# Token scores set between the parts of the value projection, and a stop for filler work at a product's end, in a recurrent-memory transformer layer

## The chip, the cores and the metric

The kernel runs on one core of a Trainium2 chip. Its time is the device time of one execution in microseconds; less is better. The core has five engines that run side by side, each through its own list of instructions in order: TensorE (PE, with its weight loads PEld), VectorE (DVE), ScalarE (ACT), GpSimd (POOL) and SyncE (SP), which here starts DMAs.

## The reference

One layer of a transformer with a recurrent memory: 2048 tokens of 640 values, in 64 segments of 32 tokens. Before each segment stand 8 memory rows, and the memory of the next segment is what attention gives for these 8 rows. Behind it comes a dense part with a squared ReLU.

```python
mem = mem0
for s in range(n_seg):                       # 64 segments, in order
    xs = x[:, s * seg_len:(s + 1) * seg_len]  # of the normalised input
    h = concatenate([mem, xs], axis=1)        # 8 + 32 rows
    q, k, v = h @ Wq, h @ Wk, h @ Wv          # 32 heads of 128
    scores = q @ k.T * scale                  # causal mask, memory seen by all
    o = (softmax(scores) @ v) @ Wo
    mem = o[:, :M]                            # the next segment's memory
    outs.append(o[:, M:])
h = x + concatenate(outs)
out = h + (relu(layernorm(h) @ w1 + b1) ** 2) @ w2 + b2
```

Segment s + 1 needs the memory of segment s, so the 64 steps form one chain.

## The kernel before, in words

The program is unrolled, and the order of each engine's instructions is that in which the Python code writes them; semaphores are added where one engine needs another's result. One call of `step(b, sp)` handles one segment s = 4b + sp. The rows that depend on the memory and the first 24 tokens ("main" rows) are handled in the step; projections of each segment's last 8 tokens ("tail" rows), which no memory needs, are prepared in blocks and used as filler.

In a step PE works through these groups. A "projection" is 20 matmuls: five chunks of the contraction, four matmuls in each, which fill the four 32-row quarters of a PSUM bank.

- Projections (line 234): q of head half 0 (`ps<-wq,hT`), k half 0 (`pk`), q half 1 (`px<-wq`), k half 1 (`ps<-wk`).
- `scores(0)` (line 495): 16 small matmuls, the scores of the memory rows for half 0, into the tile `sm`. Line 501 (DVE), 504 (ACT) and `soft2`, `soft3` (lines 510 to 529 on DVE, ACT and POOL) make the softmax of it and lay it out as `pB`.
- The value projection of half 0 (`px<-wv`), which ACT copies out in line 595, then the first chunk of half 1 (`ps1`, shown as `ps<-wv`).
- `scores(1)`, the same for half 1. It needs the transposed k of half 1 (line 485 on DVE). Its softmax ends with line 521 on DVE.
- The other four chunks of `ps1`; ACT copies the result out in line 614.
- `token_scores(0)` and `token_scores(1)` (line 587): 16 matmuls each, the scores of the 24 + 8 token rows, into a tile `sk` of their own. They need qT and kT, of which POOL puts in the tail rows (line 389). Their softmax (lines 618, 647 to 664) is wanted only in the next step.
- `values(0)` and `values(1)` (lines 537 and 542): probabilities times values for the memory rows; line 244 and 246 copy the result to `oT`.
- `pw` (line 270): 64 matmuls, the output projection of the memory rows. From it ACT and DVE make the next memory and write it, transposed, to `hT` (line 380), for which the next step's first projection waits.
- Token values of the step before (lines 421 and 426).

Filler stands in between. `portion` hands each step about 8 units; a unit is one chunk (4 matmuls) of a tail projection (`hTt`), or a tenth of a tail output projection (`wo,oTt`), and a product has 5 or 10 units. A half of the step's units goes ahead of `values(1)`: about a quarter ahead of `values(0)`, a quarter between the two, and the rest behind `pw`. `run(q, n, held, stop)` takes n units; with `stop` it breaks off when a unit ends a product.

All projections that go through `mmtile()` share three PSUM buffers: k half 1, `ps1`, `sk`, and the filler's products. A product that starts in a step takes the buffer that was filled and emptied first, in many steps that of `ps1`, and then waits for ACT's copy in line 614. `sk` is given back by line 649 on DVE, which stands behind `values(1)`.

Of the kernel before, what the change touches and what calls it, by code (L numbers as in the profile page):

```python
# [16 lines left out]
def kernel(  # L17
# [206 lines left out]
    def proj(w, by, lhs, n, ps, c0, c1):  # L224

        if by == "columns":
            wr = w[:].rearrange("p (c g j n k e) -> p c n k g j e", c=DC, g=G, n=2, j=4, k=4)
        elif by == "half":
            wr = w[:].rearrange("p (c k j n e) -> p c n k j e", c=DC, k=G, n=2, j=4)
        else:  # L230
            wr = w[:].rearrange("p (c k n f) -> p c n k f", c=DC, k=G, n=2)
        for c in range(c0, c1):
            for k in range(4):
                nc.tensor.matmul(ps[32 * k:32 * k + 32, :], lhsT=lhs(c), rhs=wr[:, c, n, k], start=(c == 0), stop=(c == DC - 1))  # L234

    def mmtile():
        return mm.tile([128, 512], F32, tag="mm", name="ps")
# [54 lines left out]
    fill, late, mid, nook = [], [], [], []  # L292

    def run(q, n, held=None, stop=False):
        while n > 0 and q:
            out = q.pop(0)()
            if out and held is not None:
                held.append(out)
                if stop:
                    break  # L300
            elif out:
                out[1]()
            n -= 1
# [10 lines left out]
    def settle(held, tails):  # L314
        for out in [o for o in held if o[0] == tails]:
            held.remove(out)
            out[1]()
# [96 lines left out]
    def token_values(s, v, vt4, po):  # L414

        sp = s % 4
        pTk, pTx = back.pop()
        for i in range(HG):
            for g in range(G):
                r = slice(32 * g, 32 * g + 32)  # L420
                nc.tensor.matmul(po[0][g][:, i * 32:(i + 1) * 32], lhsT=v[r, i * E:(i + 1) * E], rhs=pTk[r, i, :],  # L421
                                 start=(i == 0), stop=False, skip_group_check=True)
        for u in range(2):
            for g in range(G):
                r = slice(32 * g, 32 * g + 32)
                nc.tensor.matmul(po[0][g][:, u * 128:(u + 1) * 128].rearrange("p (j q) -> p j q", q=32)[:, :, 0:TL],  # L426
                                 lhsT=vt4[r, sp, u, :], rhs=pTx[r, u], start=False, stop=True, skip_group_check=True)

    def token_out(s, po):
        for h in range(2):  # L430
            gs = slice(2 * h, 2 * h + 2)
            nc.scalar.copy(out=oTg[:, gs, :, :, 0:SEG],  # L432
                           in_=po[1][h][:, :, 0:256].rearrange("p g (n j q) -> p g n j q", n=2, q=32))
        nc.gpsimd.tensor_copy(out=oTts[s // 4 % 2][:, :, s % 4 * TL:(s % 4 + 1) * TL], in_=oT[:, :, 0:TL])
# [17 lines left out]
    def step(b, sp, v=None):  # L452
        s = b * 4 + sp
        last = s == NS - 1
# [77 lines left out]
        def values(n, pB, po):  # L532
            cols = po[:, 0, 0:128]
            for j in range(4):
                i = n * 4 + j
                for k in range(4):
                    nc.tensor.matmul(cols[32 * k:32 * k + 32].rearrange("p (g i m) -> p i g m", g=G, i=4)[:, j],  # L537
                                     lhsT=v[:, i * E + 32 * k:i * E + 32 * k + 32],
                                     rhs=pB[:, :, SEG + j * M:SEG + (j + 1) * M],
                                     start=(j == 0), stop=False, skip_group_check=True)  # L540
            for k in range(4):
                nc.tensor.matmul(cols[32 * k:32 * k + 32].rearrange("p (g a) -> p g a", g=G), lhsT=vt4[:, sp, n, 32 * k:32 * k + 32], rhs=pB[:, :, 0:SEG],  # L542
                                 start=False, stop=True, skip_group_check=True)

        def values_out(n, po):
            evac(n == 1, oT[:, n * 16:(n + 1) * 16, SEG:NK], po[:, 0, 0:128].rearrange("p (a m) -> p a m", m=M))
# [28 lines left out]
        if not ready:  # L575
            ps0 = potile(0)
            proj(wv, "half", lhs, 0, ps0, 0, 2)
        sk = mmtile() if last else None

        def view():  # L580
            return sk[:, 0:HG * NK].rearrange("p (i k) -> p i k", k=NK)

        def token_scores(n):
            skv = view()
            for j in range(4):
                for g in range(G):
                    nc.tensor.matmul(skv[32 * g:32 * g + 32, n * 4 + j, :], lhsT=qT[:, n * 16 + g * 4 + j, :],  # L587
                                     rhs=kT[:, n * 16 + g * 4 + j, :], start=True, stop=True,
                                     skip_group_check=True)

        if last:
            token_scores(0)
        if not ready:
            proj(wv, "half", lhs, 0, ps0, 2, DC)
            nc.scalar.copy(out=v[:, 0:512], in_=ps0[:])
# [6 lines left out]
            pT0 = soft3(pm0)  # L602
        if not ready:
            proj(wv, "half", lhs, 1, ps1, 1, 2)
        if last:
            token_scores(1)
        if not ready:
            proj(wv, "half", lhs, 1, ps1, 2, DC)
        if not last:
            sk = mmtile()  # L610
            token_scores(0)
            token_scores(1)
        if not ready:
            nc.scalar.copy(out=v[:, 512:1024], in_=ps1[:])
        if not last:
# [1 line left out]
        def causal(skv):  # L617
            nc.vector.tensor_tensor(out=skv[:, :, M:NK], in0=skv[:, :, M:NK],
                                    in1=mask[:].unsqueeze(1).to_broadcast([128, HG, SEG]), op=ALU.add)

        held = []
# [5 lines left out]
        if last:  # L627
            run(fill, max(1, (len(fill) - 3) // 2), held, True)
            token_values(s - 1, *prevs[-2], po)
            token_out(s - 1, po)  # L630
            settle(held, True)
            run(fill, 2, held)
            settle(held, True)
            causal(skv)
        else:
            ahead = 0 if ready else (len(fill) + 1) // 2
            run(fill, ahead // 2, held)
            values(0, pT0, po[1][0])
            values_out(0, po[1][0])
            run(fill, ahead - ahead // 2, held)  # L640
            values(1, pT1, po[1][1])
            causal(skv)
            values_out(1, po[1][1])
            settle(held, True)
# [21 lines left out]
        if not last:  # L666
# [10 lines left out]
            held = []  # L677
# [236 lines left out]
    for b in range(NB):  # L914
        for sp in range(4):
# [34 lines left out]
            if 2 <= e <= NK4 + 1:  # L950
                late.insert(0, (1.15, lambda e=e: prep_stats0(e - 2), b * 4 + sp))
                mid.append(lambda e=e: prep_norm0(e - 2))
            step(b, sp, v0 if b + sp == 0 else None)

    def end_tails():
# [122 lines left out]
```

## Time and profile before

| what | value |
|---|---|
| times of three runs | 964.37, 963.79, 960.19 us; median 963.79 us |
| the profiled execution's own time | 961.72 us |
| its span (first to last instruction) | 959.9 us |
| around the span | 1.8 us |
| mean granted TensorE clock | 0.998 |
| PE busy | 927.6 us, 97% of the span |
| DVE, ACT, POOL busy | 701.8, 555.2, 312.3 us |
| step of the recurrence, for example | 452.4 to 464.3 us of the span: 11.9 us |

The page gives busy times, the chain of waits that ended last, and the costliest groups by source line. The timeline lists instructions in order of time, merged when equal ones follow each other: start, duration, engine, line, operation, tiles and shapes, count, and in brackets the idle time before with what ended it. A matmul's end is modelled; a row of 16 matmuls lasts to the modelled end of the last, so the time that a group takes from PE is the distance from its start to the start of the next PE row. "Issue" as the end of an idle time means that no semaphore explains it.

### The profile page before, as it was taken

The page shows a single profiled execution, that of the slowest core. Times are in us where ns is not written, and L with a number is a line of the kernel's source. Part 1 is how long each engine was busy: PE and PEld are TensorE (multiplying, and loading weights), DVE is VectorE, ACT ScalarE, POOL GpSimd, SP SyncE. Part 2 cuts the span into 40 slices and gives each one's busy share as a digit, 9 for nine tenths or more (in the row PEclk, how much of TensorE's full clock was granted, in tenths as well). Part 3 has the DMA queues.
Part 4 walks back from the last instruction along what each step waited for, and adds up shares of the span by engine and source line. Part 5 has one row for each costly group of instructions (what it writes and reads, how often), then busy time and mean ns, then how long its engine had stood idle before and what let it go on. Part 6 is the DMA issues. An engine that isn't in the chain of part 4 may idle for free.

```text
span 959.9 us, 55964 instructions
## 1 busy us (share of the span) xinstructions
PE 927.6 (97%) x24749; PEld 554.5 (58%) x24760; DVE 701.8 (73%) x2131; ACT 555.2 (58%) x1460; POOL 312.3 (33%) x1002
## 2 busy tenths in 40 slices
PE   5979999999999999999999999999999999999998
PEld 2436565656565656655565556666656655555555
DVE  5177887778877887877878787878787788556632
ACT  2546666666666666665666666666665665523321
POOL 2123333333333333333333333333333333353300
PEclk9999999999999999999999999999999999999999
DMA  9983201010102000100101010201020221633320
GB/s 354 403 258 66 43 16 27 16 31 13 23 19 29 16 21 24 21 25 9 36 9 31 15 31 14 32 12 33 9 31 8 53 43 21 208 101 87 94 56 28
DMA packets 65875, 56.66 MB, mean 59 GB/s; under 512 B 37384, under 2 KB 61712, under 8 KB 63712
## 3 DMA queue, kind: packets, MB, share of 16 engines
q1 hardware_dynamic: 65392, 52.74, 19.7%
q8 instruction: 194, 3.18, 1.4%
q14 instruction: 49, 0.40, 0.1%
q0 software_dynamic: 224, 0.33, 0.1%
q10 hardware_dynamic: 16, 0.01, 0.0%
HBM read 38.37 MB, written 9.44 MB: 50 GB/s over the span
## 4 chain that ended last, share of the span: by engine, by line
PE 87%; DMA 5%; DVE 3%; ACT 2%; SPq 2%; issue 1%; POOL 0%; ACTq 0%; DVEq 0%
PE ps L234 28%; PE pw L270 15%; PE px L234 13%; PE pk L234 7%; PE y L1035 6%; PE ps L983 6%; PE ps L270 3%; DMA wq<-in_A_Wq_dram 2%; PE po L421 2%; SPq L151 2%; PE po L537 2%; PE sm L495 1%; PE ps L587 1%; DMA wo<-in_A_Wo_dram 1%; PE po L542 1%
## 5 line engine op out<-in xcount | busy, mean ns | idle before, releaser
L234 PEld LDWEIGHTS <-hT 128*32 128x32 bf16 x7680 | 187.3, 96 | 179.4 <-DVE hT L380 23.0
L270 PE MATMUL pw<-wo,oT 128*32 128x320 bf16 x4224 | 160.5, 299 | 5.7 <-issue 3.3
L270 PEld LDWEIGHTS <-oT 128*32 128x32 bf16 x4224 | 120.2, 96 | 27.7 <-issue 9.4
L258 DVE STREAM_TRANSPOSE qT<-row 128x512 bf16<-128x512 bf16 x128 | 89.5, 699 | 44.7 <-ACT row L253 44.6
L234 PE MATMUL ps<-wv,hT 128*32 128x512 bf16 x1260 | 89.4, 378 | 0.0
L660 POOL TENSOR_TENSOR pkt<-ek,rk 128x64 bf16<-128x64 bf16 x64 | 19.0, 296 | 212.6 <-ACT otmp L286 142.5
L234 PE MATMUL ps<-wq,hT 128*32 128x512 bf16 x1260 | 81.6, 383 | 3.3 <-DVE hT L380 2.8
L654 ACT ACTIVATE ek<-tk 128x320 bf16<-128x320 f32 x64 | 30.1, 471 | 89.7 <-DVE tk L649 89.7
L234 PE MATMUL ps<-wk,hT 128*32 128x512 bf16 x1280 | 80.3, 379 | 0.0
L234 PE MATMUL px<-wq,hT 128*32 128x512 bf16 x1260 | 79.2, 379 | 0.0
L234 PE MATMUL px<-wv,hT 128*32 128x512 bf16 x1260 | 79.0, 378 | 0.0
L234 PE MATMUL pk<-wk,hT 128*32 128x512 bf16 x1240 | 77.9, 379 | 0.0
L991 ACT ACTIVATE wv<-ps,b1f 128x512 bf16<-128x512 f32 (+1 forms) x56 | 37.6, 672 | 67.0 <-PE ps L983 66.5
L432 ACT CAST oT<-po 128x512 bf16<-128x512 f32 x128 | 68.7, 589 | 8.2 <-PE po L426 2.5
L234 PEld LDWEIGHTS <-hTt 128*32 128x32 bf16 x1920 | 53.3, 97 | 32.3 <-issue 8.7
L441 POOL COPY qz<-qT 128x96 bf16<-128x96 bf16 x126 | 33.7, 267 | 112.0 <-DVE qT L258 112.0
L285 ACT COPY otmp<-pw 64x96 f32<-64x96 f32 (+2 forms) x129 | 28.9, 224 | 59.6 <-PE pw L270 39.0
L1035 PE MATMUL y<-wq,wk 128*128 128x320 bf16 x416 | 58.9, 299 | 0.2 <-DVE wk L992 0.2
L482 ACT CAST row<-ps 128x256 bf16<-128x256 f32 x126 | 40.8, 375 | 29.9 <-PE ps L234 29.1
L253 ACT ACTIVATE row<-ps 128x512 bf16<-128x512 f32 x93 | 54.7, 611 | 5.5 <-PE ps L234 4.4
L253 ACT ACTIVATE row<-px 128x512 bf16<-128x512 f32 x63 | 37.6, 597 | 32.2 <-PE px L234 32.2
L287 DVE TENSOR_TENSOR o<-pw,otmp 128x96 bf16<-128x96 f32 (+2 forms) x129 | 31.4, 243 | 31.5 <-ACT otmp L286 25.9
(138 smaller groups left out, 1887.5 us busy)
## 6 DMA issues: line engine op xcount, KB each, us to landing
wv<-in_A_Wv_dram SPq DMA_DIRECT2D x5, 1024.0 KB
wq<-in_A_Wq_dram SPq DMA_DIRECT2D x5, 1024.0 KB
wk<-in_A_Wk_dram SPq DMA_DIRECT2D x5, 1024.0 KB
wo<-in_A_Wo_dram SPq DMA_DIRECT2D x8, 640.0 KB
o_all<-o SPq DMA_DIRECT2D x256, 7.5 KB
vt<-vt_d SPq DMA_DIRECT2D x60, 64.0 KB
xt<-in_A_x_dram SPq DMA_DIRECT2D x19, 160.0 KB
wq<-in_B_w_dram SPq DMA_DIRECT2D x1, 2080.0 KB
```

Source lines behind the costliest of these rows:

```text
L234: nc.tensor.matmul(ps[32 * k:32 * k + 32, :], lhsT=lhs(c), rhs=wr[:, c, n, k], start=(c == 0), stop=(c == DC - 1))
L253: nc.scalar.mul(out=row, in_=ps, mul=scale)
L258: nc.vector.transpose(out=dst[:, n * 16:(n + 1) * 16, 0:32], in_=row.rearrange("p (h e) -> p h e", e=32))
L270: nc.tensor.matmul(pw[32 * j:32 * j + 32, c0:c0 + DH], lhsT=lhs(p), rhs=wov2[:, head(p), ch], start=(h == 0), stop=(h == 15))
L287: nc.vector.tensor_tensor(out=five(o[:])[:, cs], in0=blocks(0, 128, 32)[:, cs], in1=five(tmp[:])[:, cs], op=ALU.add)
L432: nc.scalar.copy(out=oTg[:, gs, :, :, 0:SEG], in_=po[1][h][:, :, 0:256].rearrange("p g (n j q) -> p g n j q", n=2, q=32))
L441: nc.gpsimd.tensor_copy(out=d.rearrange("p a (j f) -> p a j f", j=3)[:, :, :, 0:M], in_=src[:, :, 0:3, :])
L482: nc.scalar.copy(out=row[:, u * 256:(u + 1) * 256], in_=ps[:, u * 256:(u + 1) * 256])
L654: nc.scalar.activation(out=ek[:], in_=tk[:], func=ACT.Exp, scale=1.0)
L983: nc.tensor.matmul(ps[:], lhsT=w1[:, c, fc * 128:(fc + 1) * 128], rhs=hnT[:, c, :], start=(c == 0), stop=(c == DC - 1))
L991: nc.scalar.activation(out=r[:, 0:w], in_=ps[:, 0:w], func=ACT.Relu, bias=b1f[:, fc:fc + 1], scale=1.0)
L1035: nc.tensor.matmul(y[hh][:, 0:DH], lhsT=f1T[:, fc, k * 128:(k + 1) * 128], rhs=w2[:, fc, cs], start=(fc == 0 and not hf), stop=(fc == FFUL ...
```

## The change

Four edits, all in `step`:

- `sk` is taken from the three buffers ahead of `ps1`, in every step.
- `token_scores(0)` moves from behind `ps1` to between chunk 2 and chunk 3 of the value projection of half 0, ahead of `scores(1)`; `token_scores(1)` moves to between chunk 2 and chunk 3 of half 1. The last step had this order already.
- The filler ahead of `values(0)` stops when a product ends; what it left is made up between `values(0)` and `values(1)`, so that as many units as before stand ahead of `values(1)`.

```diff
-        sk = mmtile() if last else None
+        sk = mmtile()
...
-        if last:
-            token_scores(0)
+        token_scores(0)
         if not ready:
             proj(wv, "half", lhs, 0, ps0, 2, DC)
...
         if not ready:
             proj(wv, "half", lhs, 1, ps1, 1, 2)
-        if last:
-            token_scores(1)
+        token_scores(1)
         if not ready:
             proj(wv, "half", lhs, 1, ps1, 2, DC)
-        if not last:
-            sk = mmtile()
-            token_scores(0)
-            token_scores(1)
...
             ahead = 0 if ready else (len(fill) + 1) // 2
-            run(fill, ahead // 2, held)
+            left = len(fill) - ahead
+            run(fill, ahead // 2, held, True)
             values(0, pT0, po[1][0])
             values_out(0, po[1][0])
-            run(fill, ahead - ahead // 2, held)
+            run(fill, len(fill) - left, held)
             values(1, pT1, po[1][1])
```

The order of the instructions on DVE, ACT, POOL and SP is the same in both programs; PE's alone differs, with the same matmuls and weight loads.

## The prediction

> **What bounds the kernel now.** I read the page's busy times and its chain first, then the timeline of one usual step, then PE's waits over the 62 usual steps (62 to 818 us of the span).
>
> ```profile
> span 959.9 us, 55964 instructions
> PE 927.6 (97%) x24749; PEld 554.5 (58%) x24760; DVE 701.8 (73%) x2131; ACT 555.2 (58%) x1460; POOL 312.3 (33%) x1002
> PEclk9999999999999999999999999999999999999999
> PE 87%; DMA 5%; DVE 3%; ACT 2%; SPq 2%; issue 1%; POOL 0%; ACTq 0%; DVEq 0%
> ```
>
> PE is busy for 97% of the span at an undisturbed clock and carries 87% of the chain. The change keeps every matmul, so it can only gain what PE waits for, or what a packet of small matmuls costs more in one place than in another. Those few per cent lie in the middle of a step. The timeline's columns are start and duration in us, then the instruction, its count, and the idle time before:
>
> ```profile
> 456.81 0.27 PE L495 MATMUL sm<-kT,qz 128*32 128x40 bf16 x16
> 456.91 1.25 PE L234 MATMUL px<-wv,hT 128*32 128x512 bf16 x20
> 457.44 0.77 DVE L485 STREAM_TRANSPOSE kT<-row 128x256 bf16<-128x256 bf16 x2
> 457.89 0.31 POOL L389 COPY qT<-qTt 128x128 bf16<-128x128 bf16 x1
> 457.99 0.39 PE L234 MATMUL ps<-wv,hT 128*32 128x512 bf16 x4
> 458.20 0.33 PE L495 MATMUL sm<-kT,qz 128*32 128x40 bf16 x16
> 458.36 1.04 PE L234 MATMUL ps<-wv,hT 128*32 128x512 bf16 x16
> 458.59 0.20 DVE L501 TENSOR_REDUCE mx<-sm 128x1 f32<-128x40 f32 x1
> 459.08 0.56 POOL L529 COPY pB<-pT 32x64 bf16<-32x64 bf16 x2 [0.89 <-DVE pT L526]
> 459.21 0.42 PE L587 MATMUL ps<-kT,qT 128*32 128x40 bf16 x32
> 459.46 0.63 PE L234 MATMUL ps<-wk,hTt 128*32 128x512 bf16 x8
> 459.56 0.59 ACT L614 CAST v<-ps 128x512 bf16<-128x512 f32 x1
> 459.90 0.27 PE L537 MATMUL po<-pB,v 128*32 128x32 bf16 x15
> 460.06 0.62 PE L234 MATMUL ps<-wk,hTt 128*32 128x512 bf16 x8
> 460.09 0.45 DVE L521 STREAM_TRANSPOSE pB<-pm 128x256 bf16<-128x256 bf16 x1
> 460.59 0.28 PE L537 MATMUL po<-pB,v 128*32 128x32 bf16 x16
> ```
>
> A group takes from PE the distance between its start and the next group's. `scores(0)` takes 456.91 - 456.81 = 0.10 us; `scores(1)` takes 0.16, because its second half waits for line 485, which ends at 458.21; the 32 token scores take 0.25. `values(1)` starts at 460.59, 0.05 behind the end of line 521 (460.54). From the end of `scores(1)` (458.36) to `values(1)` is thus 2.23 us of softmax on DVE, ACT and POOL, and in 39 of the 62 steps, counted through the timeline, that chain and not PE's filler sets when `values(1)` starts. The weight loads show it too, as idle time put down to "issue":
>
> ```profile
> PEld L537 <- issue: 10.2, 36, 1.0
> ```
>
> **Part 1: the token scores, and the memory softmax behind them.** The 32 matmuls for 0.25 us become twice 16. A batch of 16 right behind a projection chunk costs 0.10 (`scores(0)`); as half of the 32 it costs 0.125. I take 0.10, and 0.145 as the upper end, since the second 16 of the 32 take 0.145 counted singly. So PE saves 0.04 a step on these matmuls. But `token_scores(0)` now stands ahead of `scores(1)`, and delays it by 0.10. Of that 0.05 comes back: `scores(1)` starts at about 458.30 instead of 458.20, line 485 ended at 458.21, and its 16 take 0.10 instead of 0.155. So `scores(1)` ends 0.05 later (0.00 to 0.095), and all that hangs on the softmax with it. In 51 steps the old distance is 0.153 to 0.156, in 11 it is 0.197, where nearly all comes back: 51 x 0.054 + 11 x 0.01 = **+2.9 us** for 62 steps.
>
> In the 39 chain-bound steps the time that PE saves behind `scores(1)` only becomes a longer wait before `values(1)`. In 13 others filler holds `values(1)` 0.03 to 0.13 behind the chain; there PE's saving (0.04 + 0.05 in all) counts as far as that gap allows, which from their gaps gives **-1.1 us** against the +2.9.
>
> Two new waits cost nothing while their cover holds. `token_scores(1)` needs line 389 on POOL, which ends at 458.20, and now starts at about 458.41 instead of 459.21: 0.2 us of cover remain; if POOL came 0.3 later, the remaining chunks of `ps1` behind it would be late by 0.1. `ps1` takes the third buffer, and its first matmul waits in 47 steps for ACT's line 482, which ends about 0.4 us before; behind that wait would stand `scores(1)`. DVE, ACT, POOL and SP (with its DMA issues) keep their order, and nothing is moved past them. `sk` is held longer, which matters only for the filler's choice of a buffer, below.
>
> **Part 2: the stop.** It changes the order in 9 steps, in which a new product starts ahead of `values(0)`. One of them:
>
> ```profile
> 471.36 0.41 PE L234 MATMUL ps<-wk,hTt 128*32 128x512 bf16 x4
> 471.45 0.59 ACT L614 CAST v<-ps 128x512 bf16<-128x512 f32 x1
> 472.09 0.40 PE L234 MATMUL ps<-wv,hTt 128*32 128x512 bf16 x4 [0.32 <-ACT v L614]
> 472.31 0.28 PE L537 MATMUL po<-pB,v 128*32 128x32 bf16 x16
> PE ps L234 <- ACT v L614: 2.7, 10, 0.3
> ```
>
> The new product's first chunk waits until line 614 has emptied its buffer (472.04), and `values(0)` queues behind. With the stop `values(0)` goes first, into that wait; its softmax is ready by then (line 529 on POOL ends 1.28 behind `scores(1)`: 459.64 - 458.36). `values(0)` takes 0.16 (459.90 to 460.06), less than the wait (2.7 us in 10). The wait itself stays, and late next is the same copy in line 614. Saved: 9 x 0.16 = **-1.4 us**; bounds 0 and, if the copy too came 0.04 earlier with `ps1`'s end, -1.8.
>
> Parts 1 and 2 together: 2.9 - 1.1 - 1.4 = **+0.4 us**.
>
> **Part 3: where PE stands with nothing to wait for.** The waits over the 62 steps, and one of them in the timeline with its DMA traffic (second line from the end: GB/s in 40 slices of 445 to 450 us, 0.125 us each):
>
> ```profile
> PE pw L270 <- issue: 2.8, 7, 0.6
> PE po L537 <- issue: 1.7, 2, 0.9
> PE po L426 <- issue: 0.6, 3, 0.2
> ...
> 445.34 0.33 PE L495 MATMUL sm<-kT,qz 128*32 128x40 bf16 x16
> ...
> 447.96 0.58 PE L270 MATMUL pw<-wo,oT 128*32 128x320 bf16 x10
> 449.19 2.08 PE L270 MATMUL pw<-wo,oT 128*32 128x320 bf16 x54 [0.64 <-issue]
> L270 PE MATMUL pw<-wo,oT 128*32 128x320 bf16 x3968 | 150.3, 299 | 3.2 <-issue 2.8
> GB/s 0 0 3 61 18 0 0 0 0 0 0 0 0 0 131 0 0 0 0 0 0 0 0 0 0 0 0 0 0 0 0 0 0 0 0 0 0 0 0 0
> q8 instruction: 194, 3.18, 1.4%
> ```
>
> PE breaks off within `pw` with its operands there. 194 instruction packets of 3.18 MB are 16.4 KB each, and 24749 + 24760 instructions over 194 are 255 to a packet: PE's code arrives in blocks of 256. The packet of slice 14 (446.75) is followed by PE's restart at 449.19, 2.4 us later. Counted in the program, the ten matmuls before the stop end a block that began within `scores(1)`, at about 445.36. So this block ran out in 2.9 us (448.25), and the next was there 3.8 after its start. Elsewhere 256 instructions are 128 large matmuls and last over 6 us, so only this stretch, dense in small ones, can outrun the code.
>
> What these stops cost is more than the idle time listed, since that begins at a modelled end 0.30 behind a `pw` matmul's start, of which 0.27 is no work of PE (54 of them go by in 1.8 us): 2.8 + 1.7 + 0.6 = 5.1 listed, plus 7 x 0.27 + 5 x 0.17 (the small ones), makes 7.8 us.
>
> The change pulls 64 instructions, the token scores, out of this stretch to its front. A block that ends at the same ten `pw` matmuls then begins ten matmuls before the end of the `px` value projection, 0.54 us of large matmuls (half of 457.99 - 456.91) ahead of where it began, and lasts about 3.6 us instead of 2.9. That takes nearly all of the waits at `pw` and line 537: 2.8 + 1.7 + 9 such ends = 6.7 us. The stops at line 426 (1.1 us) belong to blocks that begin with `values(1)`, which the change leaves alone. Since 3.6 is still under 3.8, I take **-6.0 us**, with 0 (no dependence on density) and -7.8 as bounds.
>
> [...]
>
> **Sum.** 961.72 (the profiled execution) + 0.4 - 6.0 = 956.1. The median of the runs lies 2.07 above that execution (963.79), so the forecast is **958.2 us**, 0.58% less. Differences under about 0.5%, 4.8 us, can't be told from none.
>
> **The rivals.** *The stops stay.* The block boundaries keep their distance of 256, and if the time from one block to the next were set by something other than the density of this stretch (PE's start of the fetch, or a fetch that slides along with the consumption), each stop would only move to another line. For it: 7 + 2 + 3 stops in 62 steps are few, and three of them lie behind the stretch. Against it: 9 of 12 lie at its end. Then only +0.4 is left: 963.79 + 0.4 = 964.2 us; the stops could also grow a little where the scores are now denser. Chance 0.33, within 0.5%. The same number comes out if the change doesn't do what it says and its two parts cancel.
>
> *The token batch is paid in full, ahead of the memory softmax* (slower). If `scores(1)` gives nothing back, because its second half waits for line 485 as it does now by some other limit (the load of weights behind a batch), its end moves by the whole batch, 0.10 to 0.145, in every step: 62 x 0.145 = 9.0, less the 2.5 of the filler-bound and stopped steps, is +6.5, and with no gain from part 3 that is 970.3 us. For it: 39 steps are bound by just this chain. Against it: line 485 ends at 458.21, before the batch would. Without part 3 this decides for slower from a delay of about 0.12 a step (7.4 - 2.5 = 4.9). Chance 0.13; with part 3's gain the same delay ends at about 964, within 0.5%.
>
> **How the numbers follow.** The forecast's case has chance 0.54, the stops that stay 0.33, the full price 0.13. In the first case the gain passes 4.8 us unless part 3 gives under 5.2, or part 1 costs 1 us more; I leave 0.03 of it to that. So faster 0.51, same 0.36, slower 0.13. The low end, 953.0, is part 3 at -7.8 with no delay of `scores(1)` and the stop at its bound (-1.1 - 1.8 = -2.9): 963.79 - 10.7. The high end, 967.0, takes in the stops that stay with a delay of 0.095 in each step (5.9 - 2.5 = +3.4). Beyond it lies the slower rival, 0.13, and beyond the low end little.
>
> **What would show it.** In the profile after: `scores(1)` takes 0.10 and its end stands 0.05 later against the start of the `px` projection; `values(1)` still starts 0.05 behind the last transpose of the softmax (line 521 before) in some 40 steps; the waits for line 614 remain, about 10, with `values(0)` ahead of them; and "issue" before `pw` and `values` falls from 9 waits to one or two. I am wrong if those waits stay or move to other lines, if `scores(1)` still takes 0.15, or if `token_scores(1)` waits for POOL's line 389.

## The result and the profile after

| kernel | median of its runs | ratio to the kernel before, 95% interval |
|---|---|---|
| before | 963.03 us (10 runs, 960.19 to 965.75) | |
| changed | 958.09 us (10 runs, 956.13 to 961.42) | 0.9953 [0.9936, 0.9970] |
| both again, another series: before | 959.97 us (31 runs) | |
| changed | 958.38 us (11 runs) | 0.9970 [0.9955, 0.9985] |

The changed kernel is faster by 0.3 to 0.5%. The forecast was 958.2 us. In the two series the changed kernel took nearly the same time; the kernel before did not (960.0 and 963.0), and that is taken up below.

The page of the changed kernel, the rows that answer to those shown before:

```profile
span 954.6 us, 55984 instructions
PE 923.6 (97%) x24760; PEld 544.0 (57%) x24760; DVE 703.6 (74%) x2131; ACT 552.3 (58%) x1460; POOL 309.5 (32%) x1002
PEclk9999999999999999999999999999999999999999
PE 80%; ACT 6%; DVE 5%; DMA 5%; SPq 2%; issue 1%; ACTq 0%
q8 instruction: 194, 3.18, 1.4%
```

The chain of waits now has 6% of ACT and 5% of DVE where it had 2% and 3%: it runs through the memory softmax in more steps. PE's waits over the same 62 steps (total us, times, longest) say the same, and show what went. First one line of before, then the changed kernel:

```profile
PE po L537 <- DVE pB L521: 0.4, 1, 0.4
...
PE po L537 <- DVE pB L521: 3.4, 15, 0.5
PE ps L234 <- DVE hT L380: 2.8, 3, 1.2
PE ps L234 <- ACT v L608: 2.4, 11, 0.2
PE pw L270 <- issue: 0.6, 2, 0.3
...
PE po L537 <- issue: 0.3, 1, 0.3
PE po L426 <- issue: 0.3, 1, 0.3
```

"Issue" had 5.1 us in 12 waits at `pw`, line 537 and line 426; it has 1.2 in 4. The wait of `values` for the softmax's last transpose (line 521) went from 0.4 us in one step to 3.4 in 15. A usual step of the changed kernel in the timeline, from `scores(0)` to `pw` (lines 608 and 594 were 614 and 595):

```profile
90.89 0.27 PE L495 MATMUL sm<-kT,qz 128*32 128x40 bf16 x16
91.00 0.60 PE L234 MATMUL px<-wv,hT 128*32 128x512 bf16 x8
91.43 0.27 PE L587 MATMUL ps<-kT,qT 128*32 128x40 bf16 x16
91.52 0.77 DVE L485 STREAM_TRANSPOSE kT<-row 128x256 bf16<-128x256 bf16 x2
91.53 0.82 PE L234 MATMUL px<-wv,hT 128*32 128x512 bf16 x12
91.97 0.30 POOL L389 COPY qT<-qTt 128x128 bf16<-128x128 bf16 x1
92.17 0.39 PE L234 MATMUL ps<-wv,hT 128*32 128x512 bf16 x4
92.39 0.27 PE L495 MATMUL sm<-kT,qz 128*32 128x40 bf16 x16
92.49 0.38 PE L234 MATMUL ps<-wv,hT 128*32 128x512 bf16 x4
92.71 0.26 PE L587 MATMUL ps<-kT,qT 128*32 128x40 bf16 x16
92.81 0.81 PE L234 MATMUL ps<-wv,hT 128*32 128x512 bf16 x12
93.45 0.60 PE L234 MATMUL ps<-wv,hTt 128*32 128x512 bf16 x8
93.72 0.58 ACT L608 CAST v<-ps 128x512 bf16<-128x512 f32 x1
93.89 0.27 PE L537 MATMUL po<-pB,v 128*32 128x32 bf16 x16
94.04 0.60 PE L234 MATMUL ps<-wv,hTt 128*32 128x512 bf16 x8
94.82 0.27 PE L537 MATMUL po<-pB,v 128*32 128x32 bf16 x16 [0.17 <-DVE pB L521]
```

Each token batch takes 0.10 us (91.43 to 91.53, 92.71 to 92.81), `scores(1)` takes 0.10 (92.39 to 92.49) instead of 0.155, since line 485 ended at 92.29, and `token_scores(1)` waits for nothing (line 389 ended at 92.27). Behind the second filler piece (94.04, eight matmuls, 0.43) PE now stands 0.35 us before `values(1)`.

And one of the nine steps with the stop: a product ends (eight `ps<-wo,oTt`), `values(0)` follows at once, and the wait for line 608 stands behind it, 12.48 us for this step before and 12.38 after.

```profile
141.79 0.45 PE L270 MATMUL ps<-wo,oTt 128*32 128x320 bf16 x8
142.05 0.58 ACT L608 CAST v<-ps 128x512 bf16<-128x512 f32 x1
142.12 0.27 PE L537 MATMUL po<-pB,v 128*32 128x32 bf16 x16
142.23 0.24 PE L542 MATMUL po<-pB,vt 128*32 128x128 bf16 x4
142.65 0.45 DVE L521 STREAM_TRANSPOSE pB<-pm 128x256 bf16<-128x256 bf16 x1
142.69 0.83 PE L234 MATMUL ps<-wq,hTt 128*32 128x512 bf16 x12 [0.23 <-ACT v L608]
```

### The profile page after: what moved, and what is told of

Its sections match the earlier page's. It is cut to its first block, busy times and chain, and to the rows that moved or that the text cites. A ratio compares the mean times of both kernels' runs of the same rounds, so it can differ in the third digit from the quotient of the medians.

```text
span 954.6 us, 55984 instructions
## 1 busy us (share of the span) xinstructions
PE 923.6 (97%) x24760; PEld 544.0 (57%) x24760; DVE 703.6 (74%) x2131; ACT 552.3 (58%) x1460; POOL 309.5 (32%) x1002
## 4 chain that ended last, share of the span: by engine, by line
PE 80%; ACT 6%; DVE 5%; DMA 5%; SPq 2%; issue 1%; ACTq 0%
PE ps L234 23%; PE pw L270 15%; PE px L234 14%; PE pk L234 7%; PE y L1030 6%; PE ps L978 6%; ACT v L594 3%; PE ps L270 2%; DMA wq<-in_A_Wq_dram 2%; PE po L421 2%; ACT em L504 2%; SPq L151 2%; DVE pm L518 2%; PE po L537 2%; DVE pB L521 2%
## 5 line engine op out<-in xcount | busy, mean ns | idle before, releaser
L234 PEld LDWEIGHTS <-hT 128*32 128x32 bf16 x7680 | 178.9, 96 | 161.2 <-DVE hT L380 24.3
L270 PE MATMUL pw<-wo,oT 128*32 128x320 bf16 x4224 | 157.7, 299 | 2.5 <-DMA wo<-in_A_Wo_dram 1.0
L234 PE MATMUL ps<-wv,hT 128*32 128x512 bf16 x1260 | 91.9, 377 | 0.0
L234 PE MATMUL px<-wv,hT 128*32 128x512 bf16 x1260 | 85.2, 377 | 0.0
L537 PEld LDWEIGHTS <-v 128*32 128x32 bf16 x2016 | 34.1, 94 | 34.7 <-issue 15.6
```

The source lines that it names most:

```text
L270: nc.tensor.matmul(pw[32 * j:32 * j + 32, c0:c0 + DH], lhsT=lhs(p), rhs=wov2[:, head(p), ch], start=(h == 0), stop=(h == 15))
```

## The experiments

The theory, an estimate of mine from the page and the traces of before: PE's code arrives in blocks of 256 instructions (255 to each of the 194 packets of queue q8), and the stretch from `scores(1)` to `pw` used a block up before the next was there (2.9 us for the block, 3.8 to PE's restart, at the stop in the prediction); the change lengthens that block's time and loses a little of it to the memory softmax. Beside PE's "issue" rows I use one count for all kernels, the code stops. Of the distance between the starts of two successive matmuls, what goes beyond the distance that nine in ten such pairs (same lines, same shape) keep to is taken, if it is over 0.1 us, if it falls within 12 instructions of the edge of a block of 256, and if the second matmul waits for no semaphore; from 62 to 816 us. The name is the theory's. Without the condition on the edge the count is 25 in the kernel before and 7 in the changed one, and 21 and 6 of these fall at one place modulo 256, within 3 instructions.

| kernel | median us | ratio to before, same series | code stops: count, us |
|---|---|---|---|
| before / again | 963.0 / 959.8 | - / 0.9990 [0.9976, 1.0004] | 21, 9.0 / 16, 7.4 |
| changed / again | 958.1 / 958.4 | 0.9953 / 0.9970 | 6, 2.3 / 7, 2.4 |
| moved scores, no stop | 959.4 | 0.9974 [0.9962, 0.9986] | 12, 4.3 |
| stop alone | 960.5 | 0.9987 [0.9972, 1.0003] | 20, 8.0 |
| scores issued twice | 986.2 | 1.0238 [1.0214, 1.0261] | 47, 23.1 |
| both batches behind `scores(1)` | 961.9 | 0.9988 [0.9971, 1.0005] | 21, 8.4 |
| only batch 0 moved | 957.7 | 0.9987 [0.9974, 1.0000] | 7, 2.0 |
| changed, a copy on DVE | 959.0 | 1.0003 [0.9991, 1.0015] | 8, 3.3 |
| before, a copy on DVE | 960.0 | 1.0016 [1.0004, 1.0027] | 16, 6.3 |
| first chunk behind `scores(1)` | 959.6 | 1.0006 [0.9995, 1.0016] | 17, 5.3 |
| changed, lines 510 and 511 exchanged | 956.7 | 0.9955 [0.9940, 0.9971] | 11, 4.5 |
| before, the same exchange | 959.4 | 0.9990 [0.9974, 1.0006] | 15, 5.7 |

Rows 3 to 6 share one series, in which the kernel before took 962.1; rows 7 to 10 share another, where it took 958.7; the last two and both "again" a third, 960.0. The medians of different series are therefore not compared below; the expectations, written ahead of the runs, do compare them. The stops are counted in one execution each, and the kernel before and its repetition show how far two executions of one program can lie apart (9.0 and 7.4 us).

**The scores without the stop, and the stop alone.**

```diff
-            left = len(fill) - ahead
-            run(fill, ahead // 2, held, True)
+            run(fill, ahead // 2, held)
...
-            run(fill, len(fill) - left, held)
+            run(fill, ahead - ahead // 2, held)
```

> Both token batches stand between the chunks as in the changed kernel; the filler has no stop, as before. Theory (the gain is PE's code stops, and the stop edit saves 0.16 us in 9 steps): 959.5 us, 1.4 above the changed kernel's 958.1, and the idle time 'issue' of PE over the usual steps stays near 1.2 us. Rival (the gain is the stop edit's, the moved scores only cost the chain): 963 us or more.

The second kernel makes the opposite edit in the kernel before.

> The kernel before with the stop edit alone. Theory: 963.0 - 1.4 = 961.6 us, 'issue' idle of PE before pw and values stays near 4.5 us (5.1 in all). Rival (the stop carries the gain): about 958 us.

The moved scores alone gave 0.26% of 962.1, 2.5 us, where 3.5 were expected (963.0 to 959.5); the stop alone 1.3 us, about as expected (1.4; its interval just takes in none), with 4.0 us of "issue" idle at `pw` and `values`. The stop doesn't carry the gain. The "issue" idle of the first is 2.3 us, between the 1.2 expected and the 5.1 of before, so the stop edit also bears on the code stops, or executions differ by that much; one trace each can't tell.

**The scores issued twice.** The test of density itself: PE has 0.33 us to spare before `values(1)`, and the 32 small matmuls of 0.25 us are put there a second time.

```diff
             proj(wv, "half", lhs, 1, ps1, 2, DC)
+        if not last and not ready:
+            token_scores(0)
+            token_scores(1)
```

> The changed kernel with the 32 token score matmuls issued a second time behind the value projection, where they stood before (the same products written again). PE has 0.33 us of wait ahead of values(1) in a usual step, which hides 0.21 of them; in some 10 steps without that wait they cost 0.2 each, 2 us. Theory (a block of 256 instructions that is used up too soon): the block that ends in pw then begins behind scores(1) and lasts 2.6 us, less than the 2.9 of before, so the stops return: 'issue' idle of 5 us or more at pw and values, time 958.1 + 2 + 6 or more, 966 to 969 us. Rival (the stops vanished because the block boundaries happen to fall elsewhere, density plays no part): 'issue' idle of 1 to 2 us, about 960 us.

It lost far more than either side said: 986.2 us, 24 above the kernel before in its series. The waits of PE and one stop in its timeline:

```profile
PE po L537 <- issue: 4.1, 7, 0.9
PE po L542 <- issue: 4.0, 6, 0.9
PE pw L270 <- issue: 3.9, 9, 0.9
PE ps L270 <- issue: 1.7, 2, 1.0
...
93.71 0.42 PE L587 MATMUL ps<-kT,qT 128*32 128x40 bf16 x32
93.96 0.63 PE L234 MATMUL ps<-wv,hTt 128*32 128x512 bf16 x8
94.40 0.20 PE L537 MATMUL po<-pB,v 128*32 128x32 bf16 x5
94.90 0.25 PE L537 MATMUL po<-pB,v 128*32 128x32 bf16 x11 [0.29 <-issue]
```

PE breaks off within `values(0)`, after 5 of 16 matmuls that all have the same operands ready. Where no stop falls a usual step takes 11.95 to 11.98 us, as in the changed kernel: there the extra matmuls themselves are free. 64 more instructions in a stretch of under 3 us raise the stops from 2.3 to 23.1 us. The 62 steps add up to 26.0 us more than in the changed kernel, so some 5 us are not stops, more than the 2 us expected for steps without spare time; what they are wasn't traced further. That speaks plainly for the theory, though its price was put far too low (966 to 969 us).

**Where the batches stand.** Behind `scores(1)`, so that the memory softmax isn't delayed; and only batch 0 ahead of it.

```diff
# both behind scores(1)
-            proj(wv, "half", lhs, 1, ps1, 2, DC)
+            if not last:
+                token_scores(0)
+            proj(wv, "half", lhs, 1, ps1, 2, 4)
+            if not last:
+                token_scores(1)
+            proj(wv, "half", lhs, 1, ps1, 4, DC)
...
# only batch 0 moved
             proj(wv, "half", lhs, 1, ps1, 2, DC)
+            if not last:
+                token_scores(1)
```

(In both, the batches are left out at their old places in all steps but the last.)

> Both token batches stand between chunks of the second half's value projection, behind scores(1): chunk 2, batch 0, chunks 3 and 4, batch 1, chunk 5; the stop is kept. The memory softmax isn't delayed any more (scores(1) takes 0.155 again, its end 0.05 earlier), but the block that ends in pw holds all 32 score matmuls again. Theory: the stops are back as before (about 5 us 'issue'), 963.0 - 1.4 for the stop - 0.3 = 961.3 us. Rival (the stops of before were chance): 958.1 less the chain's delay of about 3 us, 954 to 955 us.

> The changed kernel with token_scores(1) put back behind the second value projection; only token_scores(0) stands ahead of scores(1). Theory: the block that ends in pw still holds 32 of the 64 score instructions and begins where it does in the changed kernel, so the stops stay away ('issue' idle 1 to 2 us) and scores(1) is delayed as much: 958 us, within 1 us of the changed kernel. Rival (it takes both batches, or the spreading of the second, to be rid of the stops): 'issue' idle 3 us or more, 961 us or more.

PE's waits at `pw`, the first of both behind, the second of batch 0 alone:

```profile
PE pw L270 <- issue: 4.3, 12, 0.7
...
PE pw L270 <- issue: 0.6, 1, 0.6
```

With both behind, the stops are there (8.4 us) and the time is 961.9, next to the 961.3 expected, though no softmax is delayed. With only batch 0 moved they stay away (2.0 us) and `values(1)` starts 2.326 us behind `scores(1)`, as in the changed kernel (2.327). By the traces, moving the second batch brings nothing: what counts is that batch 0 leaves the stretch. The times say less. In this series the kernel before took 958.7, so that batch 0 alone gained only 0.13%, at the edge of the noise; the changed kernel itself didn't run in this series, and of the kernel before there is no trace from it.

**The softmax, which now sets the step.** The rest of the sum had come out some 1.6 us worse than forecast (next section), and line 511 showed why. In 60 of 62 steps of the changed kernel its second multiplication takes 0.225 us, in the kernel before in 33, and else 0.155 (the expectations below have 61 and 35). First the long form (changed kernel), then the short one (before), DVE and POOL:

```profile
93.23 0.51 POOL L529 COPY pB<-pT 32x64 bf16<-32x64 bf16 x2 [0.96 <-DVE mx L501]
93.46 0.16 DVE L510 RECIPROCAL rm<-zm 128x1 f32<-128x1 f32 x1 [0.16 <-ACT em L504]
93.54 0.23 DVE L511 TENSOR_TENSOR em<-em,same 128x32 bf16<-128x32 bf16 x1
93.80 0.48 DVE L518 SCALAR_TENSOR_TENSOR pm<-em,rm,own 128x256 bf16<-128x256 bf16 x1
...
130.12 0.56 POOL L529 COPY pB<-pT 32x64 bf16<-32x64 bf16 x2 [0.86 <-DVE pT L526]
130.34 0.16 DVE L510 RECIPROCAL rm<-zm 128x1 f32<-128x1 f32 x1
130.42 0.15 DVE L511 TENSOR_TENSOR em<-em,same 128x32 bf16<-128x32 bf16 x1
130.61 0.48 DVE L518 SCALAR_TENSOR_TENSOR pm<-em,rm,own 128x256 bf16<-128x256 bf16 x1
```

Where line 511 is long, POOL's pair of copies takes 0.51; where it is short, POOL's takes 0.56. Each takes its longer time where the other takes its shorter one. Two ways out were tried: one of the four copies given to DVE, and the two lines exchanged.

```diff
-  (nc.vector.tensor_copy, nc.scalar.copy, nc.gpsimd.tensor_copy, nc.gpsimd.tensor_copy)
+  (nc.vector.tensor_copy, nc.scalar.copy, nc.gpsimd.tensor_copy, nc.vector.tensor_copy)
```

> The changed kernel with one of the four copies of the softmax (line 529) moved from POOL to DVE, ahead of the reciprocal. Theory (in the changed kernel POOL's second copy begins 0.04 us ahead of the second multiplication of line 511 on DVE, which then takes 0.225 instead of 0.155 us in 61 of 62 steps, against 35 before, and that delays values(1)): line 511 takes 0.155 in every step, values(1) starts 2.25 us behind scores(1) instead of 2.33, 0.07 x 51 chain-bound steps: 954.5 us. Rival (line 511's length has nothing to do with POOL's copy): 958 to 959 us.

> The same move of one copy in the kernel before. Theory: 35 steps there have the long form of line 511, some 22 of them are bound by the softmax: 22 x 0.07 = 1.6 us less, 960.5 us, and the code stops stay (about 5 us of 'issue' idle). Rival: 962 us.

Line 511 is short in every step of both kernels now (mean 154 ns, 187 and 173 before), so POOL's copy was what stretched it. But nothing was won, which my expectation had overlooked: the added copy holds DVE until 1.01 us behind `scores(1)`, line 510 starts at 1.04 instead of 0.97, and line 521 ends at 2.27 as before. In the kernel before it was a loss of 0.16%, where 29 steps had the short form already; there too line 510 starts 0.08 later.

```diff
-  nc.vector.reciprocal(out=rm[:], in_=zms[n][:])
   nc.vector.tensor_tensor(out=ems[n][:, 0:SEG]..., in0=ems[n][:, 2 * SEG:]..., in1=same[:], op=ALU.mult)
+  nc.vector.reciprocal(out=rm[:], in_=zms[n][:])
```

> The changed kernel with lines 510 and 511 exchanged: the multiplication, which needs only the exponentials (0.84 us behind scores(1)), goes ahead of the reciprocal, which waits for their sum (0.93). Theory: line 518 starts 1.17 to 1.22 us behind scores(1) instead of 1.31, values(1) follows 0.09 to 0.14 earlier in the 51 steps that the softmax bounds: 4.6 us less or more, 953.5 us beside the changed kernel's 958. Rival (the softmax doesn't set the time, or DVE loses the time again on POOL's copies): 957 to 958 us.

> The same exchange in the kernel before. Theory: 39 steps are bound by the softmax, and PE has about 0.15 us of wait in them, so 0.09 each, 3.5 us less than the kernel before in the same series, with as many code stops or a few more, since the dense stretch gets shorter. Rival: no difference.

The exchange works as such: `values(1)` starts 2.27 us behind `scores(1)` instead of 2.33, 0.05 less (0.09 to 0.14 were expected), and an undisturbed step takes 11.93 instead of 11.98. The time is 956.7, 1.7 below the changed kernel in the same series, though the two intervals overlap; it is the lowest median of all. It should have been 2.7 (51 x 0.053). Even the 1.7 isn't shown: in nearly every kernel of these series the executions with a granted clock of 0.996 took 1 to 3 us longer in the mean than those with 0.998, and the two kernels had different shares of them. With 0.998 the means are 956.2 (changed) and 955.9 (exchanged), with 0.996 they are 958.7 and 957.5. The code stops rose from 2.4 to 4.5 us; by the theory a shorter softmax is a shorter block, which would explain it. In the kernel before the exchange gave 0.1%, inside the noise.

**The first chunk of `ps1` behind `scores(1)`.**

```diff
             ps1 = mmtile()
-            proj(wv, "half", lhs, 1, ps1, 0, 1)
+            if last:
+                proj(wv, "half", lhs, 1, ps1, 0, 1)
...
-            proj(wv, "half", lhs, 1, ps1, 1, 2)
+            proj(wv, "half", lhs, 1, ps1, 1 if last else 0, 2)
```

> The changed kernel with the first chunk of the second half's value projection moved behind scores(1). scores(1) then starts 0.21 us earlier and waits for line 485, as in the kernel before; its end comes 0.05 us earlier in each step, and the block that ends in pw keeps its start. Theory: 51 chain-bound steps gain 0.05 (2.6 us), the copy in line 608 comes 0.16 later and costs the 10 or so steps that wait for it 0.16 each (1.6): 957 us, stops as few as in the changed kernel. Rival (the delay of scores(1) doesn't set the time): 958.1 or, with the later copy, 959.7 us.

A miss: no gain (1.0006; the kernel with batch 0 alone, the nearest to the changed one in that series, had 0.9987). `scores(1)` did move ahead and waited for line 485 (it took 0.27), but the stops came back to 5.3 us and `values(1)` was bound by the softmax in only 30 steps instead of 51.

**Both kernels unchanged, side by side.**

> The kernel before, unchanged, for a trace of its own beside the next run: it took 963.0 and 962.1 us in two series and 958.7 in a third. Theory (the code stops differ from series to series): where it takes 959 us, 'issue' idle is 2 us or less; where it takes 962 to 963, 4 us or more. Rival (something else differs): 'issue' idle near 5 us in both.

> The changed kernel, unchanged, in the same series. Theory: 958 us in any series, 'issue' idle 1 to 1.5 us, since it has few stops to lose; so the ratio is 0.995 to 0.996 where the kernel before takes 962 to 963, and 0.999 where it takes 959. Rival (its time moves with that of the kernel before): ratio 0.995 in each, 954 us beside 959.

The second expectation held: the changed kernel takes 958.4 with 1.2 us of "issue" idle (2.4 of stops), and the ratio is 0.997 where the kernel before takes 960.0. In the first, neither side came true. The kernel before took 959.8, and its "issue" rows are neither 2 us nor near 5:

```profile
PE pw L270 <- issue: 2.8, 6, 0.7
PE po L537 <- issue: 0.9, 2, 0.5
PE po L426 <- issue: 0.4, 2, 0.3
```

That is 4.1 us instead of 5.1. Its 62 steps add up to 752.8 us instead of 755.4. Two things account for most of these 2.5 us: the code stops, 7.4 instead of 9.0, and line 511, short in 38 steps instead of 29 (9 x 0.07 = 0.6 us). That compares two executions. Why the medians of the kernel before vary from 958.7 to 963.0 between series, and so the gain of the kernels with few stops from about 0.1 to 0.5%, stays open. The last three series ran on three different chips (numbers 6, 7 and 4), so the chip itself may be the reason; no run separates it.

## Why the prediction was right, point by point

**The sum.** 956.1 was forecast for the profiled execution; it has a span of 954.6 and a time of 956.46. The 62 usual steps add up to 750.7 us instead of 755.4: -4.7, where -5.6 was worked out. That the median came within 0.1 us of 958.2 is luck. Two terms missed by some +1.6 and -0.7 us, and the 2.07 us from the profiled execution to the median came from three runs; over ten runs the kernel before has 963.03. The gain of 4.9 us just passes the 4.8 that the prediction called the least that can be told from none, and in the second series it was 1.6.

**Part 3, the code stops: -6.0 forecast, -6.7 measured** (9.0 to 2.3 by the count above, one execution each). The stops at `pw` and line 537 went nearly all. The mechanism was argued from one stop and the sizes of the packets. The runs show that the stops go with the density of the stretch: 23.1 us with the doubled scores, where it is densest, 8.4 with both batches behind `scores(1)`, 2.3 in the changed kernel. That PE waits for code there remains my inference from the packets. One sentence of the step was wrong: "pulls 64 instructions ... out of this stretch". The block that ends in `pw` holds batch 1 in either order, only batch 0 leaves it, as the kernel with batch 0 alone confirms (2.0 us of stops). The 3.6 us that were worked out are those of 32. Nor are the 3.8 us from a block's start to PE's restart, read from one stop, a fixed time: in the kernel before, 36 of the blocks went by in under 3.6 us, the shortest in 2.9, with no stop behind them (more in the last section).

**Part 1, the delayed softmax: +1.8 forecast after the credit, more measured.** `scores(1)` does take 0.10 instead of 0.155, the credit of 0.05 was right, and the rival of the full price fell. Mis-sized was what follows. The maximum (line 501) ends 0.456 us behind `scores(1)` instead of 0.438, so a dense batch gives back 0.02 less than its starts say. And in place of the short line 511 the long one came in 27 more steps, 0.07 each, of which nothing in the step's working spoke. An undisturbed step that took 11.85 or 11.92 now takes 11.98; in the 24 steps that take under 12 us in both traces that is 0.08 in the mean, 1.9 us together, and in the others stops and waits changed at the same time. The forecast took a constant chain from `scores(1)` to `values(1)`, though the trace has two lengths, 2.24 and 2.31; that step failed. `values(1)` is now bound by the softmax in 51 steps, where some 40 were forecast. In all parts 1 and 2 come to +2.0 instead of +0.4, as what the -6.7 of part 3 leaves of the -4.7; no run measures them by themselves.

**Part 2, the stop: -1.4 forecast.** Eight of the nine steps, those without a code stop, got shorter by 0.05 to 0.14, 0.11 in the mean; with the 0.05 of the delay that is the 0.16 of the forecast. The kernel with the stop alone gave 1.6 us in medians (1.3 by the ratio). The wait for the copy remains, 2.4 us in 11.

**The rivals.** That the stops only move elsewhere is refuted by the count over the whole recurrence, and by the kernel with both batches behind `scores(1)`, which has the same matmuls, 8.4 us of stops and no gain clear of noise. The slower case, a full price for batch 0, would have needed `scores(1)` to keep its 0.155.

## What to carry to other kernels

A PE that stands with all its operands ready, in a stretch of many small matmuls, may be out of code, which is what I infer here: divide the number of the engine's instructions by that of its instruction packets (255 here, read as 256), find which instruction of the program each stop falls on, and see if the stops lie whole blocks apart (21 of 25 do in the kernel before). What helped here was to spread small instructions among large ones (9.0 us of stops became 2.3), even at a small price on the chain (0.05 us a step); a shorter chain through such a stretch may give part of its gain back (4.5 us of stops with the lines exchanged, 2.4 without). Time a moved operation against both lengths of what follows it, if the rows show two (2.24 and 2.31 us here).

## What the runs showed of the hardware

All 224 code stops of the 14 traces end 2.1 to 3.0 us after the start of the newest instruction packet of queue q8, the queue taken for PE's (the latest packet that began before PE's restart). Whether PE stopped behind a short block went with when that packet started. In the kernel before, the 36 blocks that went by in under 3.6 us without a stop had it 0.28 us behind their own start (median), the 21 with a stop 0.94; in the changed kernel these are 0.70 (36 blocks) and 1.5 (6). What sets the packet's start was not looked into.

Where the block that ends in `pw` got 0.05 to 0.06 us shorter, the code stops grew by 2 to 3 us (lines exchanged 4.5, first chunk moved 5.3, against 2.4 and 2.0 in their series). One execution each is behind these numbers, and two of one program differ by 1.6 us.

A 128x32 multiplication on DVE with two operands took 0.155 us beside no copy on POOL, and 0.225 when POOL's 32x64 copy had begun some 0.04 us ahead of it; in the changed kernel it then ended 0.03 us behind the copy's end in all 60 steps. When the copy had begun only 0.03 ahead, the copy took 0.29 instead of 0.235. One of the two was late wherever they overlapped so. By the traced starts the line between the two cases lies 0.032 us behind the copy's start in the kernel before: in 27 steps with 0.027 to 0.032 the copy took its longer time, in 33 with 0.032 to 0.037 the multiplication did. What the two share there isn't shown.
